# The down projection's bfloat16 products, moved next to each other

## Chip, core and metric

The kernel runs on one core of one Trainium2 chip. The metric is the device time of one execution in microseconds (us), taken as the median of several runs. All times below are in us unless marked ns.

## What is computed

The reference is one conditioned transformer block: a layer norm with modulation, linear attention over 32 heads, a second layer norm with modulation, and a gated feed-forward network, each branch added back to x through a gate. S is 2048 tokens, D is 1024 and F is 3584; inputs and weights are bfloat16. Only the last part matters here:

```python
def _B_ref(x, w_gate, w_up, w_down):
    return _gelu(x @ w_gate) * (x @ w_up) @ w_down
...
h = _layernorm(x, axis=-1) * (1 + cb) + sb
x = x + gb * _B_ref(h, B_w_gate, B_w_up, B_w_down)
```

The change is in the last product, y @ w_down, where y is 2048 x 3584 and w_down is 3584 x 1024. This is called the down projection below.

## The kernel before

The kernel is written by hand as one program per engine. Every operation is recorded in program order with the memory that it reads and writes, in SBUF (by byte range) and in PSUM (by bank). A tracker turns each overlap into a wait: a write waits for the earlier readers and writers of the same bytes, a read waits for the last writer. Within one engine the recorded order is the order of execution. In the down projection no planner changes that order; `reorder` is applied to an earlier stretch alone.

The queues are therefore five lists: PE (matmuls, L1672 in `d_prod`), ACT, DVE, POOL, and SP, which issues the DMAs. A waiting instruction holds all that stands behind it in its own list. Some waits on SP come from DMA lanes: SP has eight lanes in rotation, and a DMA waits for the one before it on its lane.

The down projection works on pairs of token chunks, `ca` and `cb = ca + 1`, of 128 tokens each: eight pairs, numbered 0 to 7. Each pair is a two by two block product with seven products instead of eight (the scheme of Strassen and Winograd). The blocks are: two token chunks; two halves of 512 output columns; and the contraction over F split into even and odd blocks of 128 (r = 0 and 1). One product is a chain of 14 matmuls (`NDJ`) of 128x128 by 128x512.

- P1 and P2 multiply y itself with w_down itself, so both operands are bfloat16. P1 reads y of r = 0 and P2 that of r = 1.
- P5, P6, P7, P3 and P4 multiply a sum of y blocks (`d_s(ca, i)`, i = 0 to 4, L1648 on DVE and L1643 on ACT, tile `sb`) with a sum of weight blocks (`d_t`, tiles `dt` and `dh`, made once). These operands are fp32r.

Each pair has four PSUM banks, `b0` to `b0 + 3`; `b0` is 0 for even and 4 for odd pairs. The order of a pair before is P1, P5, P6, P2, P7, P3, P4, and the banks are used so:

- P1 fills b0. ACT copies it to b0 + 2 (`d_cp`, L1692).
- P5 fills b0 + 3, and ACT copies that to the SBUF tile `de` (`d_ecp`, L1698).
- P6 adds to b0 + 2. Then DVE writes b0 + 1 = b0 + 2 + de (`d_add(b0 + 1, b0 + 2)`, L1695).
- P2 adds to b0, which is then complete and is evacuated as part 0.
- P7 adds to b0 + 2. Then DVE writes b0 + 3 = b0 + 2 + de (`d_add(b0 + 3, b0 + 2)`), which is evacuated as part 3.
- P3 adds to b0 + 1, evacuated as part 1. P4 adds to b0 + 2, evacuated as part 2.

An evacuation (`evac`) is two DVE operations, times the gate (L1576) and plus the residual in tile `xq` (L1577), and one DMA to the output (L1578). `x_in` (L1568) reloads a residual tile, and `y_in` (L1571) loads one r half of y for a whole pair into tile `ya`. There is one `ya` buffer for each r, so `y_in` of the next pair, called through `y_next(r)`, waits for the last reader of that half in this pair.

The sums of the next pair are made ahead: `d_s(ca + 2, 0)` behind the evacuation after P3, `d_s(ca + 2, 1)` after P4. `d_s(ca, 2)` follows P5, `d_s(ca, 3)` follows P6 and `d_s(ca, 4)` follows P7. Two sets of `sb` buffers are shared by the five sums, so each sum also waits for the product that used its buffer.

Pair 0 is written out in `d_pair0`, with some products split because the feed-forward stage before it still runs. Pairs 1 to 7 go through `d_pair(i, hook)`; `hooks(i)` adds the work that belongs to a pair: late weight sums and two evacuations of pair 0 in pair 1, the reloads of `xq` in the others, and in pair 7 three scalings of weight sums by the gate (`t_gb`, L1652 on DVE). In pair 7 P3 is done in two parts, the second after P4 in a bank of its own.

Of the kernel before, what the change touches and what calls it, by code (L numbers as in the profile page):

```python
# [330 lines left out]
def bass_adaLN_cond__linear_attn_block__geglu_ffn__prompt_kernel(  # L331
# [18 lines left out]
    with ExitStack() as es:  # L350
# [192 lines left out]
        def pr(b):  # L543
            return [(b * 2048, (b + 1) * 2048)]

        def PS(b, c0=0, c1=512):
            return ps_all[:, b * 512 + c0: b * 512 + c1]
# [594 lines left out]
        for c_ in range(10, NCH):  # L1142
            b = seq.index(("k", c_ // 2 * 2, 0)) - (9 if c_ % 2 else 12)
# [6 lines left out]
        for c_ in range(8, NCH, 2):  # L1150
            b = seq.index(("k", c_, 0)) - 3
# [422 lines left out]
        def evac(c_, k, b, c0, c1):  # L1574
            n = 2 * (c_ % 2) + k
            sch.op(V, lambda e: e.tensor_tensor(PS(b), PS(b), GBB[:, c0:c1], ALU.mult), prd=pr(b), pwr=pr(b), rd=R_GBB, note=f"x2a c{c_}.{k}")  # L1576
            sch.op(V, lambda e: e.tensor_tensor(XQ[n][:, :], PS(b), XQ[n][:, :], ALU.add), prd=pr(b), rd=r_xq(n), wr=r_xq(n), note=f"x2b c{c_}.{k}")  # L1577
            sch.dma(Q, lambda e: e.dma_start(out_v[:, c_, c0:c1], XQ[n][:, :]), rd=r_xq(n), note=f"out{c_}.{k}")  # L1578
# [29 lines left out]
        def d_t(i, q):  # L1608
            j0, j1 = 0, 2
            w = WDT[q][:, 2 * j0:2 * j1, :].rearrange("p (j r) d -> p j r d", r=2)  # L1610
            b = lambda r, cc: (w[:, :, r, cc * 512:(cc + 1) * 512], r_wh(q, r, cc, f"wd{q}", j0, j1))
            t32 = lambda k: (dt_ap(q, k, j0, j1)[0].bitcast(f32), dt_ap(q, k, j0, j1)[1])
            dst, wr = dt_ap(q, i, j0, j1)
            if i == 3:
                src, rd = b(1, 1)
                sch.op(A, lambda e: e.activation(dst, src, ACTF.Copy), rd=rd, wr=wr, note=f"dtcp {q}")
                return
            (in0, r0), (in1, r1) = ((b(0, 1), b(0, 0)), (b(1, 1), t32(0)), (b(1, 1), b(0, 1)), None, (b(1, 0), t32(1)))[i]
            if i == 4:
                in0, in1 = (t_.rearrange("p j (h c) -> p j h c", h=2) for t_ in (in0, in1))  # L1620
            sch.op(V, lambda e: e.tensor_tensor(dst, in0, in1, ALU.subtract), rd=r0 + r1, wr=wr, note=f"dtsum {q}.{i}")

        def nj(ca):
            return NJP[ca // 2]
# [10 lines left out]
        def d_s(ca, i, hs=(0, 1)):  # L1635
            cb, n = ca + 1, nj(ca)
            for j0, j1 in (((0, min(n, NSJ)), (NSJ, n))[h] for h in hs):
                if j0 >= j1:
                    continue
                dst, wr = ds_ap(ca, i, j0, j1)  # L1640
                if i == 4:
                    src, rd = y_ap(cb, 1, j0, j1)
                    sch.op(A, lambda e, dst=dst, src=src: e.activation(dst, src, ACTF.Copy), rd=rd, wr=wr, note=f"dscp {cb}")  # L1643
                    continue
                s_ = lambda k: (ds_ap(ca, k, j0, j1)[0].bitcast(f32), ds_ap(ca, k, j0, j1)[1])
                (in0, r0), (in1, r1), op = ((y_ap(cb, 0, j0, j1), y_ap(cb, 1, j0, j1), ALU.add), (s_(0), y_ap(ca, 0, j0, j1), ALU.subtract),
                                            (y_ap(ca, 0, j0, j1), y_ap(cb, 0, j0, j1), ALU.subtract), (y_ap(ca, 1, j0, j1), s_(1), ALU.subtract))[i]
                sch.op(V, lambda e, dst=dst, in0=in0, in1=in1, op=op: e.tensor_tensor(dst, in0, in1, op), rd=r0 + r1, wr=wr, note=f"dssum{i} {cb}")  # L1648
# [6 lines left out]
        def d_prod(ca, b0, k, own=None, js=None):  # L1655
            b = b0 + {1: 0, 2: 0, 5: 3, 6: 2, 7: 2, 4: 2, 3: 1}[k] if own is None else own
            i = {1: None, 2: None, 5: 0, 6: 1, 7: 2, 3: 3, 4: 4}[k]
            o = None
            js = range(nj(ca)) if js is None else js
            for j in js:  # L1660
                q, jj = divmod(j, 2)
                dst = PS(b)
                if i is None:
                    l_, rl = y_ap(ca, k - 1, j, j + 1)
                    r_, rr = WDT[q][:, 2 * jj + k - 1, 0:512], r_wh(q, k - 1, 0, f"wd{q}", jj, jj + 1)
                else:
                    l_, rl = ds_ap(ca, i, j, j + 1)
                    t_, rr = dt_ap(q, i, jj, jj + 1)
                    r_ = t_[:, 0]
                    if i == 4:  # L1670
                        dst = dst.rearrange("p (h c) -> p h c", h=2)
                o = sch.op(T, lambda e, l_=l_, r_=r_, j=j, dst=dst: e.matmul(dst, l_[:, 0, :], r_, start=(k in (1, 5) or own is not None) and j == js[0], stop=j == js[-1], skip_group_check=True),  # L1672
                           rd=rl + rr, pwr=(pr(b) if j == js[0] else ()), note=f"down P{k} c{ca} j{j}", overwrite_ok=True)
            pset_writer(b, o)
# [16 lines left out]
        def d_cp(dst, src, note):  # L1691
            sch.op(A, lambda e: e.activation(PS(dst), PS(src), ACTF.Copy), prd=pr(src), pwr=pr(dst), note=note)  # L1692
# [11 lines left out]
        def d_pair0(hook):  # L1704
            parts = parts_of(0)
            for k in (2, 6, 5, 0, 7, 3, 13, 11, 12, 4):
                n = k - 10 if k > 10 else k
                if k in (0, 11, 12, 13):
                    down(*parts[n], list(range(2 * nj(0), NFC)), n != 2, True)
                    hook(k)  # L1710
                    continue
                d_prod(0, 0, k)
                if k == 6:
                    d_cp(1, 2, "ducp")
                elif k == 5:
                    d_ecp(3)
                    d_add(1, 1)
                elif k == 7:
                    d_add(3, 2)
                hook(k)  # L1720

        def d_pair(i, hook):
            ca, b0 = 2 * i, i % 2 * 4
            last = i == 2 * CPG - 1
            parts = parts_of(i)

            def y_next(r):
                if not last:
                    y_in(i + 1, r)

            for k in (1, 5, 6, 2, 7, 3, 4):
                if last and k == 3:
                    d_prod(ca, b0, 3, None, range(6, NDJ))
                    evac_part(*parts[1])
                    continue
                d_prod(ca, b0, k)
                if k == 1:
                    d_cp(b0 + 2, b0, "dpcp")
                elif k == 5:
                    d_ecp(b0 + 3)  # L1740
                    d_s(ca, 2)
                elif k == 6:
                    d_add(b0 + 1, b0 + 2)
                    d_s(ca, 3)
                    y_next(0)
                elif k == 2:
                    evac(*parts[0])
                elif k == 7:
                    d_add(b0 + 3, b0 + 2)
                    d_s(ca, 4)  # L1750
                    y_next(1)
                    evac(*parts[3])
                elif k == 3:
                    evac(*parts[1])
                    d_s(ca + 2, 0)
                else:
                    if not last:
                        d_s(ca + 2, 1)
                    evac(*parts[2])
                    if last:  # L1760
                        d_prod(ca, b0, 3, 0, range(6))
                        evac_sum(*parts[1][:2], 0, *parts[1][3:])
                hook(k)
# [62 lines left out]
        for n in range(12):  # L1826
            q, i = divmod(n, 4)
# [56 lines left out]
        def hooks(i):  # L1884
            def hook(k):
                more = i + 1 < 2 * CPG
                if i == 1:
                    if k == 1:
                        d_t(2, 5)
                        d_t(2, 6)  # L1890
                    if k in (6, 2, 7):
                        d_t(4, {6: 4, 2: 5, 7: 6}[k])
                    if k in (6, 7):
                        n = 1 if k == 6 else 2
                        evac(*parts_of(0)[n])
                        x_in(1, n)
                else:
                    if k == 1:
                        x_in(i, 0, 3, 1)
                    elif k == 5:  # L1900
                        x_in(i, 2)
                    if not more and k in (5, 6):
                        for q in {5: (0, 1), 6: (2,)}[k]:
                            t_gb(q)
            return hook

        d_pair0(hook0)
        for i in range(1, 2 * CPG):
            d_pair(i, hooks(i))

# [74 lines left out]
```

## Time and profile before

| | |
|---|---|
| Median of 3 runs | 782.6 (782.56 to 783.66) |
| Span of the profiled execution | 780.9 |
| Median above that span | 1.7 |
| PE busy | 770.2 (99%) |
| DVE busy | 645.9 (83%) |
| ACT busy | 374.6 (48%) |
| Down projection, L1672 | matmuls from 598.6 to 777.6 of the span |
| Mean granted TensorE clock | 1.000 |

The profile tells one execution by its span, from the first instruction to the last. Its own device time is not listed apart from the runs; the runs are some 1.7 above the span, which is what lies around it. Engine rows give busy time and the share of the span. PE is the matmul row and PEld the weight-load row of TensorE; each matmul has one weight load, which normally runs while the matmul before it is at work. Ends of matmuls are modelled, so the spacing of starts is the better measure.

### The profile page before, as it was taken

The page shows a single profiled execution, that of the slowest core. Times are in us where ns is not written, and L with a number is a line of the kernel's source. Part 1 is how long each engine was busy: PE and PEld are TensorE (multiplying, and loading weights), DVE is VectorE, ACT ScalarE, POOL GpSimd, SP SyncE. Part 2 cuts the span into 40 slices and gives each one's busy share as a digit, 9 for nine tenths or more (in the row PEclk, how much of TensorE's full clock was granted, in tenths as well). Part 3 has the DMA queues.
Part 4 walks back from the last instruction along what each step waited for, and adds up shares of the span by engine and source line. Part 5 has one row for each costly group of instructions (what it writes and reads, how often), then busy time and mean ns, then how long its engine had stood idle before and what let it go on. Part 6 is the DMA issues. An engine that isn't in the chain of part 4 may idle for free.

```text
span 780.9 us, 10753 instructions
## 1 busy us (share of the span) xinstructions
PE 770.2 (99%) x3825; PEld 496.2 (64%) x3883; DVE 645.9 (83%) x964; ACT 374.6 (48%) x629; POOL 47.5 (6%) x126
## 2 busy tenths in 40 slices
PE   8999999999999999999999999999999999999998
PEld 4444445666445667667676767667676576677766
DVE  6699988897899878787989888888989888676767
ACT  2497743242466487878755555555555211111111
POOL 2031300000321011100000000000000000000000
PEclk9999999999999999999999999999999999999999
DMA  9879749939999358867353865535356334443331
GB/s 284 256 167 252 158 91 215 255 80 196 203 287 231 82 138 212 230 175 215 99 145 108 250 211 172 148 96 161 97 147 221 111 127 139 144 141 114 126 125 60
DMA packets 196940, 130.22 MB, mean 167 GB/s; under 512 B 69516, under 2 KB 182420, under 8 KB 195864
## 3 DMA queue, kind: packets, MB, share of 16 engines
q1 hardware_dynamic: 196872, 129.55, 62.4%
q8 instruction: 30, 0.49, 0.3%
q14 instruction: 22, 0.18, 0.1%
q10 hardware_dynamic: 16, 0.00, 0.0%
HBM read 92.55 MB, written 23.35 MB: 148 GB/s over the span
## 4 chain that ended last, share of the span: by engine, by line
PE 95%; SPq 2%; DMA 1%; DVE 1%; issue 1%; ACT 0%; DVEq 0%; ACTq 0%
PE ps_all L1458 45%; PE ps_all L1672 21%; PE ps_all L895 7%; PE ps_all L934 7%; PE ps_all L1283 7%; PE ps_all L880 5%; PE ps_all L1593 1%; SPq L598 1%; DMA wmq<-in_w_mod_dram 1%; SPq L603 1%; DMA h1T<-xh 0%; PE ps_all L913 0%; PE ps_all L1201 0%; PE ps_all L1240 0%; DVE h1T L724 0%
## 5 line engine op out<-in xcount | busy, mean ns | idle before, releaser
L1458 PE MATMUL ps_all<-ss,tp 128*128 128x512 f32 x896 | 214.3, 396 | 0.0
L1458 PEld LDWEIGHTS ps_all<-ss,tp 128*128 128x128 f32 x896 | 168.3, 188 | 37.8 <-DVE ss L1413 0.2
L1672 PE MATMUL ps_all<-dt,sb 128*128 128x512 f32 x424 | 102.5, 398 | 0.0
L1481 ACT ACTIVATE ge<-ps_all 128x512 f32<-128x512 f32 x112 | 64.1, 597 | 73.8 <-DVE ps_all L1469 62.1
L1458 PE MATMUL ps_all<-h2a,wt 128*128 128x512 bf16 x421 | 95.7, 379 | 1.8
L1672 PEld LDWEIGHTS ps_all<-dt,sb 128*128 128x128 f32 x424 | 79.6, 188 | 18.5 <-DVE sb L1648 0.3
L1476 DVE TENSOR_TENSOR ps_all<-ps_all,es 128x512 f32<-128x512 f32 x54 | 37.6, 699 | 49.4 <-ACT es L1466 49.0
L1488 DVE TENSOR_TENSOR ys<-ge,ps_all 128x512 bf16<-128x512 f32 x112 | 74.4, 684 | 3.8 <-PE ps_all L1672 0.5
L1458 PEld LDWEIGHTS ps_all<-h2a,wt 128*128 128x128 bf16 x448 | 38.0, 98 | 57.3 <-ACT ps_all L1463 16.9
L1433 DVE TENSOR_TENSOR tp<-wt 128x1024 fp32r<-128x1024 bf16 x56 | 68.1, 1217 | 1.8 <-DMA wt<-in_B_w_up_dram 1.8
L1433 DVE TENSOR_TENSOR tp<-wt,tp 128x1024 fp32r<-128x1024 bf16 x56 | 68.2, 1218 | 0.0
L934 PE MATMUL ps_all<-h1T,wq 128*128 128x512 bf16 x256 | 56.7, 379 | 0.0
L880 PE MATMUL ps_all<-wk,h1T 128*128 128x512 bf16 x239 | 55.3, 379 | 1.1 <-DMA wk<-in_A_wqkv_dram 0.5
L1283 PE MATMUL ps_all<-w,pq 128*128 128x512 bf16 x249 | 55.7, 379 | 0.5 <-issue 0.2
L1458 PE MATMUL ps_all<-ar,tp 128*128 128x512 f32 x224 | 55.5, 390 | 0.0
L869 ACT ACTIVATE eb<-ps_all 128x512 f32<-128x512 f32 x64 | 36.3, 594 | 37.6 <-PE ps_all L880 16.0
L1672 PE MATMUL ps_all<-wd,ya 128*128 128x512 bf16 x199 | 47.5, 380 | 0.7
L1458 PEld LDWEIGHTS ps_all<-ar,tp 128*128 128x128 f32 x224 | 42.1, 188 | 8.9
L1463 ACT ACTIVATE ps_all<-ps_all 128x512 f32<-128x512 f32 x56 | 32.6, 582 | 26.8 <-PE ps_all L1458 26.5
L934 PEld LDWEIGHTS ps_all<-h1T,wq 128*128 128x128 bf16 x256 | 25.0, 98 | 30.0
L1283 PEld LDWEIGHTS ps_all<-w,pq 128*128 128x128 bf16 x256 | 24.6, 98 | 30.3 <-issue 1.1
L1643 ACT ACTIVATE sb<-ya 128x896 fp32r<-128x896 bf16 (+1 forms) x16 | 14.5, 913 | 58.8 <-PE ps_all L1672 58.8
(141 smaller groups left out, 976.3 us busy)
## 6 DMA issues: line engine op xcount, KB each, us to landing
wt<-in_B_w_gate_dram SPq DMA_DIRECT2D x28, 512.0 KB, 4.0
wt<-in_B_w_up_dram SPq DMA_DIRECT2D x28, 512.0 KB, 5.2
scr_y<-ys SPq DMA_DIRECT2D x28, 512.0 KB, 3.2
ya<-scr_y SPq DMA_DIRECT2D x14, 896.0 KB, 4.9
rb<-scr_rd SPq DMA_DIRECT2D x32, 256.0 KB, 6.0
wd<-in_B_w_down_dram SPq DMA_DIRECT2D x7, 1024.0 KB, 7.6
wmst<-in_w_mod_dram SPq DMA_DIRECT2D x6, 1024.0 KB, 6.2
wmq<-in_w_mod_dram SPq DMA_DIRECT2D x8, 512.0 KB, 7.5
```

What stands on the lines that cost most here:

```text
L869: sch.op(A, lambda e: e.activation(EB[i][:, :], PS(bank), ACTF.Exp), prd=pr(bank), wr=rng, note=f"{note}.exp")
L880: o = sch.op(T, lambda e, dc=dc: e.matmul(PS(bank), H1[sg][:, ci, dc, :], W_[:, dc, jg * 512:(jg + 1) * 512], start=(dc == 0), stop=(dc == ...
L895: o = sch.op(T, lambda e, c_=c_: e.matmul(PS(bank, 0, n), PK[c_][:, g * P:(g + 1) * P], xrow(c_, o_, o_ + n), start=(c_ == 0), stop=(c_ == ...
L934: o = sch.op(T, lambda e, dc=dc: e.matmul(PS(b), WQ[:, dc, qc * P:(qc + 1) * P], H1[sg][:, :, dc, :], start=(dc == 0), stop=(dc == NDC - 1 ...
L1283: last[half] = sch.op(T, lambda e, g=g, half=half: e.matmul(PS(b0 + half), PQ[sg][:, g, ci * P:(ci + 1) * P], W2[:, g, half * 512:(half + ...
L1433: sch.op(V, lambda e: e.tensor_tensor(TP[k][:], in0, in1 if k in (0, 2) else in1[:], ALU.subtract), rd=r0 + r1, wr=r_tp(k), deps=[x1_ops[7 ...
L1458: o = sch.op(T, lambda e, l_=l_, r_=r_, dc=dc: e.matmul(PS(b), l_, r_, start=fresh and dc == 0, stop=dc == ND2 - 1, skip_group_check=True) ...
L1463: sch.op(A, lambda e: e.activation(PS(BB + t), PS(BA + t), ACTF.Copy), prd=pr(BA + t), pwr=pr(BB + t), note="pcp")
L1476: sch.op(V, lambda e: e.tensor_tensor(PS(BC + t), PS(BC + t), ES[t][:, :], ALU.add), prd=pr(BC + t), rd=r_2k(OFF_ES[t], f"es{t}"), pwr=pr( ...
L1481: sch.op(A, lambda e: e.activation(GE[i][:, :], PS(b), ACTF.Gelu_apprx_tanh), prd=pr(b), wr=r_2k(OFF_GE[i], f"ge{i}"), note="gelu")
L1488: sch.op(V, lambda e: e.tensor_tensor(YS[s_][:, 2 * h:2 * h + 2, t, :], q(GE[i][:, :]), q(PS(b + 1)), ALU.mult), rd=r_2k(OFF_GE[i], f"ge{i ...
L1672: o = sch.op(T, lambda e, l_=l_, r_=r_, j=j, dst=dst: e.matmul(dst, l_[:, 0, :], r_, start=(k in (1, 5) or own is not None) and j == js[0] ...
```

## The change

The order of a pair becomes P5, P6, P7, P2, P1 of the next pair, P3, P4. P1 and its copy `d_cp` form a function of their own, `d_open(i)`. It is called for pair 1 ahead of the loop, and in pair i after P2 for pair i + 1; in pair 7 it is left out. P2 and the next P1 stand next to each other on PE as one run of 28 bfloat16 matmuls.

With this the evacuation of part 0 and `y_next(1)` move to the step of P2, behind P7; the evacuation of part 3 stays at P7. In the hooks the two last weight sums of r = 2 in pair 1 move out to the call ahead of the loop, the sums d_t(4, ...) follow the new order, and the reloads of `xq` move from the steps of P1 and P5 to those of P5 and P6. The number of instructions on every engine is the same.

```diff
+        def d_open(i):
+            b = i % 2 * 4
+            d_prod(2 * i, b, 1)
+            d_cp(b + 2, b, "dpcp")
+
         def d_pair(i, hook):
 ...
-            for k in (1, 5, 6, 2, 7, 3, 4):
+            for k in (5, 6, 7, 2, 1, 3, 4):
+                if last and k == 1:
+                    continue
                 if last and k == 3:
                     d_prod(ca, b0, 3, None, range(6, NDJ))
                     evac_part(*parts[1])
                     continue
+                if k == 1:
+                    d_open(i + 1)
+                    continue
                 d_prod(ca, b0, k)
-                if k == 1:
-                    d_cp(b0 + 2, b0, "dpcp")
-                elif k == 5:
+                if k == 5:
                     d_ecp(b0 + 3)
                     d_s(ca, 2)
                 elif k == 6:
                     d_add(b0 + 1, b0 + 2)
                     d_s(ca, 3)
                     y_next(0)
-                elif k == 2:
-                    evac(*parts[0])
                 elif k == 7:
                     d_add(b0 + 3, b0 + 2)
                     d_s(ca, 4)
+                    evac(*parts[3])
+                elif k == 2:
                     y_next(1)
-                    evac(*parts[3])
+                    evac(*parts[0])
 ...
                 if i == 1:
-                    if k == 1:
-                        d_t(2, 5)
-                        d_t(2, 6)
-                    if k in (6, 2, 7):
-                        d_t(4, {6: 4, 2: 5, 7: 6}[k])
+                    if k in (6, 7, 2):
+                        d_t(4, {6: 4, 7: 5, 2: 6}[k])
 ...
                 else:
-                    if k == 1:
+                    if k == 5:
                         x_in(i, 0, 3, 1)
-                    elif k == 5:
+                    elif k == 6:
                         x_in(i, 2)
 ...
         d_pair0(hook0)
+        d_open(1)
+        d_t(2, 5)
+        d_t(2, 6)
         for i in range(1, 2 * CPG):
             d_pair(i, hooks(i))
```

## The prediction

> **What bounds the kernel.** All times are in us. I read the page first: span, engine shares, chain.
>
> ```profile
> span 780.9 us, 10753 instructions
> PE 770.2 (99%) x3825; PEld 496.2 (64%) x3883; DVE 645.9 (83%) x964; ACT 374.6 (48%) x629; POOL 47.5 (6%) x126
> PE 95%; SPq 2%; DMA 1%; DVE 1%; issue 1%; ACT 0%; DVEq 0%; ACTq 0%
> ```
>
> TensorE sets the end: 95% of the chain is PE, and the down projection (L1672, from 598.6 to 777.6) has hardly a wait in it. So the change pays only by what it takes from PE's own stream, and costs whatever wait it puts into it. Next, the weight loads of pair 2 in the timeline (start, duration, count):
>
> ```profile
> 654.98 2.70 PEld L1672 LDWEIGHTS ps_all<-wd,ya 128*128 128x128 bf16 x14 [0.26 <-issue]
> 657.80 6.35 PEld L1672 LDWEIGHTS ps_all<-dt,sb 128*128 128x128 f32 x28
> 664.18 3.13 PEld L1672 LDWEIGHTS ps_all<-dh,sb 128*128 128x128 f32 x14
> 667.58 2.71 PEld L1672 LDWEIGHTS ps_all<-wd,ya 128*128 128x128 bf16 x14 [0.26 <-issue]
> ```
>
> These are P2, then P7 and P3, then P4, then P1 of pair 3. VectorE in the same pair, with the wait in brackets:
>
> ```profile
> 652.48 2.08 DVE L1648 TENSOR_TENSOR sb<-ya 128x896 fp32r<-128x896 bf16 x2
> 655.25 0.70 DVE L1695 TENSOR_TENSOR ps_all<-ps_all,de 128x512 f32<-128x512 f32 x1 [0.68 <-PE ps_all L1672]
> 655.85 2.08 DVE L1648 TENSOR_TENSOR sb<-ya,sb 128x896 fp32r<-128x896 bf16 x2
> ...
> 661.44 0.70 DVE L1695 TENSOR_TENSOR ps_all<-ps_all,de 128x512 f32<-128x512 f32 x1 [1.73 <-PE ps_all L1672]
> ```
>
> The row at 655.25 decides the case. It is d_add(b0+1, b0+2): it reads the bank b0+2 that P6 has just filled, and P7 may write that bank only when it has been read. Today P2 (654.98 to 657.80) writes another bank in that time and hides the add. In the new order P7 follows P6 at once.
>
> **Saved: six bfloat16 runs.** In one run the starts of bfloat16 matmuls are 0.216 apart, those of fp32r 0.2266. A pair of 28 and 70 is 6.05 + 15.86 = 21.91 at those pitches; from P1 of pair 2 (645.54) to P1 of pair 3 (667.58) it is 22.04. The 0.13 is what two runs cost at their edges, 0.065 each. Pairs 1 to 7 have 14 such runs today and 8 after (the last keeps P2 alone, the first opens with P1): 6 x 0.065 = 0.39 saved. Bounds 0.2 and 0.6.
>
> **Term 1: P7 waits for the add, seven times.** P6's last matmul starts at 654.75 (PE timeline) and the add 0.496 later; it takes 0.700. For how PE restarts behind a DVE wait, the trace has one clean row, after the sum that ends at 608.96 + 1.08 = 610.05:
>
> ```profile
> 608.96 1.08 DVE L1648 TENSOR_TENSOR sb<-ya 128x896 fp32r<-128x896 bf16 x1
> 610.10 0.30 PEld L1672 LDWEIGHTS ps_all<-dt,sb 128*128 128x128 f32 x2 [0.30 <-DVE sb L1648]
> ```
>
> The load starts 0.053 after the DVE end, and the second matmul starts 0.337 after the load (610.44). So P7's second matmul comes 0.496 + 0.700 + 0.053 + 0.337 = 1.586 after P6's last one, against 2 x 0.227 = 0.454: a stall of 1.13, and 7 x 1.13 = 7.91. Bounds per stall 0.9 (the add and two short hops) and 1.3. In pair 1 the add starts at 633.21 with 0.18 of idle time before it, waiting for PE, so DVE is free there too.
>
> [...]
>
> **Term 2: the last pair's queue on DVE.** Its add stands behind two scalings (L1652):
>
> ```profile
> 752.77 0.70 DVE L1576 TENSOR_TENSOR ps_all<-ps_all,gbb 128x512 f32<-128x512 f32 x1 [0.94 <-PE ps_all L1672]
> 755.48 2.09 DVE L1648 TENSOR_TENSOR sb<-ya,ya 128x896 fp32r<-128x896 bf16 x2 [1.21 <-DMA ya<-scr_y]
> ...
> 763.21 2.35 DVE L1652 TENSOR_TENSOR dt<-dt,gbb 128x1024 fp32r<-128x1024 f32 x2
> 765.48 0.69 DVE L1695 TENSOR_TENSOR ps_all<-ps_all,de 128x512 f32<-128x512 f32 x1
> ```
>
> From d_s(0) at 755.48 to the add is 10.00, 0.22 of it a wait for PE: 9.78 of queue. With P1 gone from the head of the pair, d_s(0) follows the evacuation of P3 directly: 752.77 + 0.80 + 0.80 = 754.37 (both steps as at 645.49, 646.28 and 647.06), 2.02 after P4's first load at 752.35. The add can start 11.80 after that load, while P4, P5 and P6 (3.173 each) plus 0.496 would allow 10.02: 1.78 late, all on PE. Bounds 1.3 and 2.2. Pairs 2 to 6 have no scalings (2.27 less): ready at 9.53, 0.5 to spare.
>
> **Term 3: SP's order in pair 1.** y_next(1) moves behind P2, and with that past the output of xq_145, the output of xq_144 and the reload of xq_144, which waits until that output has landed. SP works in order:
>
> ```profile
> 638.39 0.34 SPq L1578 DMA_DIRECT2D out_dram<-xq  x1
> 640.17 0.32 SPq L1568 DMA_DIRECT2D xq<-scr_x  x1
> 640.54 0.43 SPq L1578 DMA_DIRECT2D out_dram<-xq  x1
> 641.08 0.36 SPq L1571 DMA_DIRECT2D ya<-scr_y  x1
> ```
>
> Today the ya load goes at 641.08. After it, counting DVE from 633.21 through d_s(3), d_t, an evacuation, the second add, an evacuation, d_t and evac of pair 0's part 2, xq_144 is done at about 643.04; its output lands and releases the reload 1.78 later (638.39 to 640.17), the ya load goes 0.55 after that, at 645.4, lands 4.8 later (median of L1571) at 650.2; d_s(0)'s first half then takes 0.09 + 1.09 and 0.05 to PE: 651.4. P5 of pair 2 would start at 648.36 + 1.13 = 649.5, the same products lying ahead of it. So 2.0 of wait, bounds 0.5 and 3.5 (landing 3.4 to 7.3). In later pairs only one output stands ahead of that load, and it lands 2.5 before its use.
>
> **At nothing.** d_cp behind the early P1 (0.58 on ACT) has P3, P4 and P5 as cover, 9.5; without it P6 would wait 0.6. y_next(0) is issued 9.6 after P4's first load and needed by the early P1 at 17.1: 4.8 fits, and the longest, 7.3, just does. The reloads of xq (2.6 to land) have two products and more. d_s(1) has P5 instead of P1 and P5: two halves of 1.0 behind d_s(0), done at 6.0 for 6.35. The tail after P3 of the last pair is unchanged.
>
> **Sum.** 7.91 + 1.78 + 2.0 - 0.39 = 11.3: span 780.9 to 792.2. The sum is made against the profiled execution's span; the median of the runs, 782.6, is 1.7 above it, which I carry over: 793.9.
>
> **Rivals.** (a) Only term 1 is paid, because DMA lands sooner and DVE catches up: 7.91 - 0.39 = 7.5, 790.1. For it: these are chains of six to ten rows. Chance 0.20. (b) P5's first half waits in pairs 3 to 7 as well: d_s(0)a ends 2.02 + 1.09 + 0.05 = 3.16 after P4's first load, and P5 wants it at 3.17. Any slip goes on PE; at 0.4 each it is 5 x 0.4 = 2.0, 795.9. Against: DVE's rows repeat within 0.02. Chance 0.10. (c) The last pair's stall of 2.9 halves the clock for the following product: +3.2, 797.1. The windows view shows 1.00 from 18 on, and the longest gap there, 1.03 from one load's start to the next at 20.04, did not lower it; no longer one is in the trace. Chance 0.03. [...] (d) Faster: the switch of type is the real price, and the removed runs give back more than their edges show. That decides only from (7.91 + 1.78 + 2.0 + 1.6) / 6 = 2.2 per run, where it gives 781.0; the rows allow 0.065. Chance 0.02. (e) The add does not hold P7 back: only 0.39 is left, 782.2, no change. It would need the add done while P6 still runs; it starts 0.5 after P6's last matmul. Chance 0.02. That the order is not changed is excluded: in the program P7 stands right behind P6 in pairs 1 to 7.
>
> **Numbers.** The forecast has 0.63. About 0.2%, 1.6, is what a measurement can tell from no change. Range 789.6 to 796.4: it takes in (a), (b) and the bounds of the terms. Faster 0.02, same 0.02, slower 0.96.
>
> **What would show it.** Right: PEld idle rows on L1672 with DVE ps_all L1695 as releaser, 7 of them, about 1.1 each and near 2.9 in the last pair; one of about 2 on DVE sb L1648 at P5 of pair 2; the bfloat16 runs as x28; PE busy unchanged but for the edges. Wrong: P7's loads following P6's at 0.227, or PEld waits on ya, or a clock below 1.00 before the end.

## The result, and the profile after

The changed kernel takes 794.44 us (793.22 to 797.5, 4 runs) against 782.76 for the kernel before (782.56 to 783.66, now with a fourth run): ratio 1.0151, 95% interval 1.0132 to 1.0171. It is slower by 11.7. The forecast was 793.9, in a range of 789.6 to 796.4. All times are in us.

The four runs differ by the TensorE clock that was granted: 793.87 and 793.22 at 1.000, 795.01 at 0.998, and 797.5 at 0.996. The last is the profiled one, with a span of 795.7; the two at 1.000 have spans of 792.1 and 791.4. The page of that profile:

```profile
span 795.7 us, 10760 instructions
PE 776.0 (98%) x3829; PEld 498.9 (63%) x3883; DVE 645.3 (81%) x964; ACT 374.6 (47%) x629; POOL 47.0 (6%) x126
PE 93%; DMA 3%; DVE 2%; SPq 1%; issue 1%; DVEq 0%; ACT 0%
```

DVE and ACT do the same work as before; on the chain PE falls from 95% to 93% and SP's queue from 2% to 1%, while DMA rises from 1% to 3% and DVE from 1% to 2%. The waits of the weight loads in the down projection (total, times, longest), which before held no wait on L1695, say who:

```profile
PEld ps_all L1672 <- DVE ps_all L1695: 10.5, 7, 2.8
PEld ps_all L1672 <- DVE sb L1648: 2.5, 2, 2.2
PEld ps_all L1672 <- DMA xq<-scr_x: 1.0, 4, 0.3
```

Seven waits on the add, one for each of pairs 1 to 7, and one of 2.2 on a sum. The third row is hardly a DMA wait: these are four starts of a bfloat16 run, 0.26 each, the same 0.26 that the profile of before put down to "issue". The timeline of the loads in pair 2 answers to that shown of before:

```profile
651.94 7.82 PEld L1672 LDWEIGHTS ps_all<-dt,sb 128*128 128x128 f32 x28 [2.21 <-DVE sb L1648]
661.05 3.05 PEld L1672 LDWEIGHTS ps_all<-dt,sb 128*128 128x128 f32 x14 [1.28 <-DVE ps_all L1695]
664.36 5.73 PEld L1672 LDWEIGHTS ps_all<-wd,ya 128*128 128x128 bf16 x28 [0.26 <-issue]
```

P5 and P6 are the first row, P7 the second, the merged run the third. The wait of 1.28 in front of P7 costs PE less than that: these loads of fp32r take 0.188 and start 0.227 apart, so 0.04 lies between them in any case, and the second load of P7 follows the first after 0.11 and not 0.227. From P6's last load to P7's second load it is 1.13 more than two pitches, and this is what "stall" means below. It is 1.13 in pairs 1 to 6 each, 2.62 in pair 7, and 2.05 in front of P5 of pair 2.

DVE in pair 2 and in the last pair:

```profile
660.30 0.70 DVE L1695 TENSOR_TENSOR ps_all<-ps_all,de 128x512 f32<-128x512 f32 x1 [2.00 <-PE ps_all L1672]
...
767.79 2.08 DVE L1648 TENSOR_TENSOR sb<-ya,ya 128x896 fp32r<-128x896 bf16 x2
775.20 2.36 DVE L1652 TENSOR_TENSOR dt<-dt,gbb 128x1024 fp32r<-128x1024 f32 x2
777.47 0.69 DVE L1695 TENSOR_TENSOR ps_all<-ps_all,de 128x512 f32<-128x512 f32 x1
```

In pair 2 the add waits for P6 and ends at 661.00; P7's load starts at 661.05. In the last pair the add has no wait of its own: it starts when the scalings are through. SP in pair 1:

```profile
638.65 0.34 SPq L1578 DMA_DIRECT2D out_dram<-xq  x1
640.43 0.32 SPq L1568 DMA_DIRECT2D xq<-scr_x  x1
640.79 2.92 SPq L1578 DMA_DIRECT2D out_dram<-xq  x2
645.11 0.33 SPq L1568 DMA_DIRECT2D xq<-scr_x  x1
645.55 0.37 SPq L1571 DMA_DIRECT2D ya<-scr_y  x1
```

The load of y goes out at 645.55, where it went at 641.08 before, behind two outputs and the reload that waits for the second of them.

The windows view (bounds; length, PE busy; granted clock after POOL) shows what the sum did not have:

```profile
649.90:653.30 3.40, 1.61 (x8) 1.14 (x7) 2.50 (x3) 0.00 (x0) 0.00 (x0) 1.00 0.18 62
653.30:656.70 3.40, 3.40 (x10) 2.62 (x9) 3.30 (x5) 0.00 (x0) 0.00 (x0) 0.50 0.00 0
776.20:779.60 3.40, 1.38 (x6) 1.17 (x7) 3.40 (x5) 0.00 (x0) 0.00 (x0) 1.00 0.18 60
779.60:783.00 3.40, 3.40 (x10) 2.39 (x8) 1.69 (x2) 0.95 (x1) 0.00 (x0) 0.50 0.00 0
```

Behind each of the two long stalls PE ran at half clock for one stretch of 3.41: eight matmuls at a pitch of 0.427 instead of 0.227, 1.6 lost.

### The profile page after: what moved, and what is told of

Its sections match the earlier page's. It is cut to its first block, busy times and chain, and to the rows that moved or that the text cites. A ratio compares the mean times of both kernels' runs of the same rounds, so it can differ in the third digit from the quotient of the medians.

```text
span 795.7 us, 10760 instructions
## 1 busy us (share of the span) xinstructions
PE 776.0 (98%) x3829; PEld 498.9 (63%) x3883; DVE 645.3 (81%) x964; ACT 374.6 (47%) x629; POOL 47.0 (6%) x126
## 4 chain that ended last, share of the span: by engine, by line
PE 93%; DMA 3%; DVE 2%; SPq 1%; issue 1%; DVEq 0%; ACT 0%
PE ps_all L1458 44%; PE ps_all L1672 19%; PE ps_all L895 7%; PE ps_all L934 7%; PE ps_all L1283 7%; PE ps_all L880 6%; DMA xq<-scr_x 2%; PE ps_all L1593 1%; DMA wmq<-in_w_mod_dram 1%; DVE sb L1648 1%; DVE ps_all L1695 0%; PE ps_all L913 0%; SPq L598 0%; PE ps_all L1201 0%; DMA out_dram<-xq 0%
## 5 line engine op out<-in xcount | busy, mean ns | idle before, releaser
L1672 PE MATMUL ps_all<-dt,sb 128*128 128x512 f32 x424 | 106.5, 406 | 9.3 <-DVE ps_all L1695 7.5
L1672 PEld LDWEIGHTS ps_all<-dt,sb 128*128 128x128 f32 x424 | 81.1, 193 | 31.0 <-DVE ps_all L1695 10.5
L1576 DVE TENSOR_TENSOR ps_all<-ps_all,gbb 128x512 f32<-128x512 f32 x31 | 21.6, 697 | 31.8 <-PE ps_all L1672 31.5
L1672 PE MATMUL ps_all<-wd,ya 128*128 128x512 bf16 x203 | 45.8, 379 | 0.6
```

## Experiments

The theory has three waits and a small gain: the add between P6 and P7 (seven stalls), the DVE queue ahead of it in the last pair, SP's order in pair 1, and 0.39 from six saved runs. The half clock behind long stalls comes on top. The rival for the first is that P7 pays for something else, such as its own sums or the change of product.

**SP's order.** The reload of xq_144 goes behind the load of y:

```diff
-                        x_in(1, n)
+                        if n == 1:
+                            x_in(1, n)
+                    if k == 2:
+                        x_in(1, 2)
```

> The changed kernel with one reload of xq_144 in pair 1 issued after y_next(1) instead of ahead of it; nothing else. Theory (SP's order): the 2.05 us wait of PE ahead of P5 of pair 2 goes, and with it the stretch of half clock behind it where it occurred; the seven waits on the add stay. Where the clock holds, 791.4 us against 793.4 for the changed kernel, and up to 793.0 with one stretch of half clock at the end. Rival (the load of y is late by itself, whatever stands ahead of it): the wait stays at about 2 us and the time at 793.2 to 797.5.

793.56 (792.06 to 794.24), ratio 1.0133 (1.0119 to 1.0147). Its profile, of a run at clock 1.000, shows first SP and then the waits of the weight loads:

```profile
643.17 0.38 SPq L1571 DMA_DIRECT2D ya<-scr_y  x1
```

```profile
PEld ps_all L1672 <- DVE ps_all L1695: 10.5, 7, 2.8
PEld ps_all L1672 <- DVE sb L1648: 0.8, 2, 0.5
```

The load goes 2.4 earlier and the stall ahead of P5 falls from 2.05 to 0.39, with no half clock behind it: the mechanism is right. It does not vanish, since two outputs still stand ahead of the load. The median is 0.6 above the expected upper bound: 0.39 stayed, and the three runs without a profile have a clock of 0.998, the size of one stretch of half clock; that it follows the last pair's stall of 2.62 is likely but not seen.

**DVE's queue in the last pair.** The scalings one step later:

```diff
-                    if not more and k in (5, 6):
-                        for q in {5: (0, 1), 6: (2,)}[k]:
+                    if not more and k in (6, 7):
+                        for q in {6: (0, 1), 7: (2,)}[k]:
```

> The changed kernel with the scalings L1652 of the last pair recorded one step later, behind the add after P6 instead of ahead of it. Theory (DVE's queue): the last pair's stall falls from 2.6 us to the 1.13 of the others, 1.5 less, and no half clock follows it; the wait ahead of P5 of pair 2 stays. 791.9 us where the clock holds, up to 793.6 with one stretch of half clock. Rival (the last pair waits for something else, such as its sums): 2.6 us stay.

793.17 (792.71 to 794.48), ratio 1.0135 (1.012 to 1.0151). The median is within what was expected, but the two runs at clock 1.000 miss the 791.9 expected for them: they took 792.71 and 793.33 with spans of 790.9 and 790.6, so the second lies 2.7 above its span, where 1.8 is usual. What takes the longer time outside the span is not shown. In the profile all seven waits are now alike, and no half clock follows:

```profile
PEld ps_all L1672 <- DVE ps_all L1695: 9.0, 7, 1.3
PEld ps_all L1672 <- DVE sb L1648: 2.2, 2, 1.9
```

The clock of that profile is 0.999, where one stretch of half clock would make it 0.998. The last stall is 1.13, so the 1.49 on top of it came from the scalings alone.

**Both together.** The two edits in one kernel.

> Both edits together: only the seven waits on the add and the six saved runs are left. Theory: 782.8 + 7 x 1.13 - 0.39 + 0.3 for restarts = 790.6 us, and the granted clock is 1.000 in every run, since no wait is over 1.2 us. Rival for the clock (many short waits lower it as well): a clock below 1.000 in some runs and 792 us or more in those.

790.78 (790.51 to 791.7), ratio 1.0103 (1.0089 to 1.0116), and a clock of 1.000 in all four runs, against 0.996 to 1.000 for the changed kernel. What is left is the seven stalls of 1.13 (7.9), 0.30 ahead of P5 of pair 2, and the gain: 7.7 over the kernel before on the same chip (783.10).

**The early opening without the merge.** P2 goes back between P6 and P7, P1 stays early:

```diff
-            for k in (5, 6, 7, 2, 1, 3, 4):
+            for k in (5, 6, 2, 7, 1, 3, 4):
...
                     d_s(ca, 4)
+                    y_next(1)
                     evac(*parts[3])
                 elif k == 2:
-                    y_next(1)
```

and the weight sums d_t(4, ...) follow P6, P2 and P7 again.

> The early opening alone: the next pair's P1 stays ahead of P3, but P2 is back between P6 and P7, so there are 14 bfloat16 runs as before the change. Theory (the read of bank b0 + 2 is what P7 waits for, and any product on another bank hides it): no PE wait on the add, 782.3 to 783.5 us. Rival 1 (the early opening itself costs, by its load of y or its banks): PE waits on ya ahead of P1, and 1 to 10 us more. Rival 2 (the stall belongs to the merged run): would also give 783, but then a merged run elsewhere stalls too.

783.25 (782.58 to 784.17), ratio 1.0003 (0.9994 to 1.0011): no difference from before. The loads of pair 2 are P2, P7 and P1 again, with only the 0.26 at each bfloat16 start between them:

```profile
654.59 2.71 PEld L1672 LDWEIGHTS ps_all<-wd,ya 128*128 128x128 bf16 x14 [0.26 <-issue]
657.41 3.17 PEld L1672 LDWEIGHTS ps_all<-dt,sb 128*128 128x128 f32 x14
660.85 2.71 PEld L1672 LDWEIGHTS ps_all<-wd,ya 128*128 128x128 bf16 x14 [0.26 <-issue]
```

One pair has a stall of 0.45 on ya ahead of P1. Beyond that, opening the next pair early costs nothing here; all of the loss comes from P7 right behind P6 and from what moved with P2.

**A later add.** The add after P6 goes behind d_s(3):

```diff
-                    d_add(b0 + 1, b0 + 2)
                     d_s(ca, 3)
+                    d_add(b0 + 1, b0 + 2)
```

> The changed kernel with the add after P6 recorded behind the two halves of d_s(3) instead of ahead of them. Theory (P7 waits for the add): each stall grows by the DVE work that now stands ahead of the add, 1.8 us in pair 1, 1.6 in pairs 2 to 6, 2.0 in pair 7, 11.7 in all: 805 us where the clock holds. Rival (P7 waits for its sums d_s(2) or pays for the weight load): no change, 793.2 to 797.5. For the clock: stalls of about 2.7 in five pairs and 4.6 in the last. [...]

809.97 (807.85 to 811.58), ratio 1.0346 (1.0328 to 1.0365). The waits of its profile:

```profile
PEld ps_all L1672 <- DVE ps_all L1695: 20.9, 7, 4.8
```

The stalls grow to 2.84 in pair 1, 2.36 to 2.69 in pairs 2 to 6 and 4.63 in pair 7, 19.9 in all against 9.4 in the changed kernel. P7 follows the add, not its own sums. The growth of 10.5 was expected as 11.7: in pairs 3 to 5 it is 1.23 each and not 1.6. The profiled run has a clock of 0.989 over a span of 809.8, the size of five stretches of half clock, and the other runs have 0.989 to 0.993: a stall of 2.36 was followed by half clock as well (its windows are in the last section).

**A shorter add.** The add after P6 on 128 columns; three quarters of that sum are left out.

```diff
-                    d_add(b0 + 1, b0 + 2)
+                    d_add(b0 + 1, b0 + 2, 128)
```

> The changed kernel with the add after P6 done on 128 of its 512 columns, which leaves three quarters of that sum out. Theory (the add's own time is on PE's path): from 128x896 in 1.08 us and 128x128 in 0.285 an element column costs 0.00104, so the add falls from 0.70 to about 0.30 and each stall from 1.13 to 0.73: 7 x 0.40 = 2.8 less, 790.6 us where the clock holds. Rival (the wait is a fixed cost of changing the product, or waits for other work): stalls stay at 1.13.

792.33 (792.04 to 792.96), ratio 1.0124 (1.011 to 1.0138).

```profile
PEld ps_all L1672 <- DVE ps_all L1695: 7.7, 7, 2.4
```

The add falls from 0.70 to 0.294, and the stalls of pairs 1 to 6 from 1.13 to 0.73, one for one: the add's own time is on the path. In the last pair the wait is 0.40 shorter too (2.8 to 2.4), but the stall falls only from 2.62 to 2.28. Three of the four runs, the profiled one among them, have a clock of 0.998, the size of one stretch of half clock, which is most of the distance to the 790.6 expected with a whole clock. The fourth, at 1.000, has the shortest span, 789.4, and yet took 792.96, 3.6 more; what takes that time is not shown.

**The merge with cover.** To see what the merge is worth by itself, the run of 28 is put between P6 and P7, where it hides the add. For that P1's y must be there sooner, so the loads of y go in halves, y_next(0) follows P5, y_next(1) follows P7, and the evacuation after P4 goes behind d_s(2):

```diff
-                    y_in(i + 1, r)
+                    y_in(i + 1, r, 0, NSJ)
+                    y_in(i + 1, r, NSJ, NDJ)
-            for k in (5, 6, 7, 2, 1, 3, 4):
+            for k in (5, 6, 2, 1, 7, 3, 4):
...
                     d_s(ca, 2)
+                    y_next(0)
+                    if i > 1:
+                        evac(*parts_of(i - 1)[2])
...
```

In pair 1 the two evacuations of pair 0 move to P5 and P6, and their reloads to P7.

> The merged run placed between P6 and P7 (P5, P6, P2, next P1, P7, P3, P4), with the next y loads split into halves and recorded as soon as their last reader is, and the evacuation after P4 recorded behind d_s(2), so that y is free sooner. Theory: the run of 28 hides the add, no PE wait on it; if y lands in time only the six saved runs are left, 782.8 - 0.4 = 782.4 us, faster than before by 0.05%. Rival (P1 is now too early for its y, which is only released by d_s(2) after P5): PE waits on ya of 0.3 to 1 us in six pairs, 784 to 788. Second rival (a run of 28 costs something by itself): 783 or more with no wait in the rows.

784.36 (783.92 to 785.44), ratio 1.0021 (1.0012 to 1.0031). Neither the theory nor its rivals had this: PE has no wait on the add and none on ya, but one of 1.8 ahead of P5 of pair 2, a stall of 1.61. In DVE's timeline an evacuation waits for a reload that I had moved too late, and holds the sums behind it:

```profile
648.26 0.69 DVE L1577 TENSOR_TENSOR xq<-ps_all,xq 128x512 bf16<-128x512 f32 x1 [1.95 <-DMA xq<-scr_x]
648.86 2.08 DVE L1648 TENSOR_TENSOR sb<-ya,ya 128x896 fp32r<-128x896 bf16 x2
```

One change mends it, the reload of xq_143 at P6 (the diff is against the kernel just shown):

```diff
-                    if k == 7:
-                        x_in(1, 1, 2)
+                    if k in (6, 7):
+                        x_in(1, 1 if k == 6 else 2)
```

> The run of 28 between P6 and P7 as before (P5, P6, P2, next P1, P7, P3, P4), with the reload of xq_143 in pair 1 issued one product earlier. In the run before this one the only wait of PE left in pairs 1 to 7 was 1.6 us ahead of P5 of pair 2, behind an evacuation that waited for this reload. Theory: it goes, and only the six saved runs are left: 784.4 - 1.6 = 782.8 us, 0.02 to 0.05% under before, which is less than the runs can tell apart; from the first to the last weight load of the down projection 178.4 us against 178.8 before. Rival (a run of 28 costs something by itself): no wait in the rows and yet 783.5 us or more.

782.54 (782.26 to 783.35) against 783.02, ratio 0.9995 (0.9986 to 1.0004): not to be told from the kernel before. The waits left are short:

```profile
PEld ps_all L1672 <- DMA ya<-scr_y: 0.8, 2, 0.6
PEld ps_all L1672 <- DVE sb L1648: 0.7, 2, 0.4
```

They cost 0.25 of stall each and eat the 0.39: from the first to the last load of the down projection it is 178.87, against 178.78 before and the 178.4 expected. In a pair without a wait the saved run can be read by itself:

```profile
698.86 5.73 PEld L1672 LDWEIGHTS ps_all<-wd,ya 128*128 128x128 bf16 x28 [0.26 <-issue]
...
720.84 5.73 PEld L1672 LDWEIGHTS ps_all<-wd,ya 128*128 128x128 bf16 x28 [0.26 <-issue]
```

From one merged run to the next it is 21.974 in the trace, against 22.040 from P1 to the next P1 in the kernel before: one bfloat16 run less in a pair saves 0.066. So the best form of the merge, of those tried, is worth nothing that can be measured, and no version here beats the kernel before.

## Why the prediction was right, step by step

| Step | Predicted | Measured |
|---|---|---|
| Term 1, P7 waits for the add | 7 x 1.13 = 7.91 | 7 x 1.13, and 0.03 more behind each |
| Term 2, scalings in the last pair | 1.78 | 1.49 |
| Term 3, SP's order ahead of P5 of pair 2 | 2.0 | 2.05 |
| Six saved runs | 6 x 0.065 = 0.39 | 0.066 a run where no wait hides it |
| Span at clock 1.000 | 792.2 | 792.1 and 791.4 |
| Half clock | rival, 0.03 | in 2 of 4 runs, 1.6 a stretch |

Term 1 is shown twice over: it follows the add when the add is made later or shorter, and it goes when bfloat16 products on another bank stand between P6 and P7. The chain from one row each (0.496, 0.700, 0.053, 0.337) came out to the hundredth. What the term left out is small: the 70 fp32r loads between two merged runs take 17.29 with both edits and 16.13 where the merged run hides the add, so a wait costs 1.16. The other 0.03 is in P7's first matmuls after the wait, up to 0.236 apart.

Term 2 is 0.29 too large. The step that was off is the 0.80 from the evacuation's second operation to d_s(0), taken from pair 1, where d_s(0) had a DMA to wait for. In the last pair y had landed long before, and it took 0.61 (767.18 to 767.79). The other 0.10 is the queue, 9.68 instead of 9.78.

Term 3 was right in its mechanism and, with bounds of 0.5 to 3.5, also by chance to 0.05: y went out at 645.55 for the 645.4 worked out. The profile names DMA out_dram as the releaser of the sum that waited there, though the buffer that it reads is the y load's: the last piece of that load landed at 650.71, and the sum started at 650.80.

That the whole sum fits as well as it does is in part luck: Term 1 is 0.2 too small over seven waits and Term 2 0.29 too large. The forecast of 793.9 also holds no half clock, while the median of 794.44 lies between a run with it and one without.

Rival (b) did not come: in pairs 3 to 7 there is no stall ahead of P5. Rival (c) was given 0.03, and half clock came about in two of four runs, in another size than its 3.2: one stretch costs 1.6, and in the profile it also followed the 2.05 in pair 2, which I had not listed as a place. The forecast had left it out of the sum. The chance of 0.03 was too low for its evidence: a longest gap of 1.03 that did no harm says nothing of one of 2.6. That PE busy would stay the same was wrong: it rose from 770.2 to 776.0, and it is 776.5 with both edits, where the clock was whole. Part of this is in the recording. The early opening without the merge takes no longer than the kernel before, and its row says 773.8, with 3883 matmuls recorded and not 3825. Ends of matmuls are modelled as well, and a last matmul before a wait shows its full 0.39; the row can't be read for a change of 1%.

## What to carry to other kernels

A product that is placed between two others may be there to cover a read of their shared accumulator. Before two products on one bank are put next to each other, follow the chain last matmul, reader, next load: here it cost 1.13 for a reader of 0.70, seven times, against 0.066 for a saved run. And of a step that is moved, list every DMA and what stands before it now on its queue: the one load that moved behind a reload cost nearly as much as two of the stalls.

## What the runs showed of the hardware

The granted clock of TensorE fell to 0.50 behind some waits of about 2 and more, and behind none of 1.13 in the profile of the changed kernel or with both edits, where four runs have 1.000. In the profile of the changed kernel the two stretches of half clock last 3.41 each and start at 653.32 and 779.61, 126.29 apart, which is 37 times that length. In the stretches read here half clock went with how long PE was idle within the 3.41 just before. In the later-add kernel, two stalls of the same size, in stretches whose borders are whole multiples of 3.413 from the start of half clock at 690.25:

```profile
686.84:690.25 3.41, 1.32 (x7) 1.06 (x7) 2.08 (x3) 0.00 (x0) 0.00 (x0) 1.00 0.95 313
690.25:693.66 3.41, 3.41 (x10) 2.61 (x8) 0.00 (x0) 0.95 (x1) 0.00 (x0) 0.50 0.12 41
710.73:714.14 3.41, 2.10 (x10) 1.41 (x8) 3.41 (x4) 0.00 (x0) 0.00 (x0) 1.00 0.71 208
714.14:717.55 3.41, 2.62 (x11) 2.17 (x12) 0.73 (x2) 0.61 (x1) 0.00 (x0) 1.00 0.66 253
```

Both stalls are 2.36. The first lies within one stretch, leaves PE 1.32 of work in it and is followed by half clock; the second is cut by the border of two stretches, leaves 2.10 and 2.62, and is not. In the profile of the changed kernel the stretches ahead of the two of half clock have 1.79 and 2.02 of PE idle, so 1.79 of 3.41 was enough there; no other such stretch of the down projection has more than 0.86, which the stalls of 1.13 leave, and none of those was followed by half clock. With the scalings later, the stretch that holds most of the stall ahead of P5 of pair 2 has 1.44 and was not followed by it either:

```profile
649.48:652.89 3.41, 1.97 (x9) 1.35 (x8) 2.75 (x3) 0.00 (x0) 0.00 (x0) 1.00 0.19 65
652.89:656.30 3.41, 3.41 (x17) 2.81 (x16) 3.31 (x5) 0.60 (x1) 0.00 (x0) 1.00 0.00 0
```

So a stall of 2 was followed by half clock in some runs and not in others: the four runs of the changed kernel have clocks of 1.000, 1.000, 0.998 and 0.996, and two stretches of 1.6 are most of the spread from 793.2 to 797.5. Where between 1.44 and 1.79 the border lies was not tried.
